# Decode attention with a gated MLP on one core: part of an output-weight block in eight-lane transfers, VectorE operations on whole K tiles

## The chip, the cores and the metric

The kernel runs on one core of a Trainium2 chip. The metric is the device time of one execution in microseconds (us); lower is better. A core has five engines that run side by side, each in the order of its own program: TensorE (PE, matmuls; PEld is its weight load), VectorE (DVE), ScalarE (ACT), GpSimd (POOL) and SyncE (SP), which here issues nearly all transfers. Sixteen DMA engines move data between HBM and SBUF, the on-chip memory of 128 partitions (lanes). Matmul results go to PSUM.

## The reference

For four sequences (B = 4) with one new token each: layer norm, attention over a cache of 4096 keys and values with 32 heads of 128 elements, and beside it a small gated MLP; both are added to the input.

```python
xn = _layernorm(x, axis=-1)
return x + _A_ref(xn, A_k_cache, A_v_cache, A_wq, A_wo) + _B_ref(xn, ...)

# _A_ref
q = (x @ wq).reshape(B, Sq, Hq, Dh).transpose(0, 2, 1, 3)
scores = jnp.einsum('bhqd,bhkd->bhqk', q, k) * Dh ** (-0.5)
p = _softmax(scores, axis=-1)
o = jnp.einsum('bhqk,bhkd->bhqd', p, v)
return o.transpose(0, 2, 1, 3).reshape(B, Sq, Hq * Dh) @ wo

# _B_ref
z = _gelu(jnp.einsum('bsd,df->bsf', x, w_in))
z2 = _layernorm(z[..., Fh:], axis=-1)
g = jnp.einsum('ts,bsf->btf', w_sp, z2) + b_sp[None, :, None]
return jnp.einsum('bsf,fd->bsd', z[..., :Fh] * g, w_out)
```

The caches are bfloat16, 4 x 32 x 4096 x 128 each: 134 MB of keys and 134 MB of values, all read once. wo is 4096 x 640.

## The kernel before

Four heads of one sequence make a tile: 4 x 4096 rows of 128 elements, laid out as 128 lanes x 128 rows x 128 elements (4 MB, 32 KB a lane). There are 32 K tiles and 32 V tiles. Tile i belongs to head group i // 4 (eight groups) and sequence i % 4. The main loop makes one turn per K tile.

**Loads.** Five SBUF slots (`KV_SLOTS`) hold K and V tiles. `pump` issues the next loads of a fixed list on SyncE's queue, which alternates V and K (twice, at turns 24 and 28, an extra K comes earlier). In turn i two loads are issued: the V tile that takes the slot freed by this turn's `blocks`, then the K tile that takes the slot freed by this turn's `sums`. SyncE waits for each slot in that order. The output weights wo come in eight blocks of 128 lanes x 2560 elements (5,120 bytes a lane); `load_wo` issues block i // 4 at the end of turns 2, 6, 10, 14, 18 and 22, behind that turn's V and K, and the last two after the loop. Two buffers hold them.

**A turn.** The order on PE, DVE, ACT and SP is written out by hand, and each engine follows it. For K tile i:

- `product` (VectorE, L457): the tile times the query, in place, in two halves of 64 rows of 128 elements (8192 elements a lane each).
- `fold_half` (VectorE, L466): adds the upper 64 elements of each row to the lower 64, for each half (4096 elements).
- `sums` (TensorE, L475): eight matmuls with the identity for each half, which add the 64 elements down to 8 in PSUM (`ps_s`, two buffers of one half each).
- `row_sums` (VectorE, L486): reduces these 8 to one score, for each half.

The second half's row sums are read in the next turn, behind that turn's first product. There also come, for tile i - 1: `lane_max` (VectorE, L495), `lay_max` (ScalarE, L501), `spread_max` (TensorE, L508), `head_max` (VectorE, L515, the negated maximum nb), and `exps`: an exponential on ScalarE (L524), then the product of the weights with a head mask on GpSimd (L533, tile pm, 512 elements a lane). Until turn 24 the V tile that is used in turn i is tile i - 1: `blocks` (TensorE, L548, 32 matmuls) multiplies pm with it. Behind every second tile come a copy to SBUF on ScalarE (L558) and `gather` (L569, eight small matmuls). On TensorE the second half's `sums` stand behind `blocks` and `gather`. From turn 26 on `blocks` is one turn further behind, in the last turn three.

When a head group is complete (turns 4, 8, ... 24), `group_den` (GpSimd L593, TensorE L600, VectorE reciprocal L602) and `group_norm` (VectorE, L607) work out the normalised output within that turn; on VectorE they stand ahead of the next turn's product. `group_turn`, `group_pick` (VectorE L627 and L635, next turn) and `group_proj` (L647) carry it through wo into `out_ps`, where the MLP's result is added too. The last V tile comes in four pieces, the last wo block in four.

VectorE's instructions of one turn, in order:

```python
product(i, 0); row_sums(i - 1, 1); lane_max(i - 1)
# group_pick of a group that the turn before has completed
fold_half(i, 0); head_max(i - 1)
product(i, 1)
# group_den's reciprocal
row_sums(i, 0); fold_half(i, 1)
# group_norm
```

Of the kernel before, what the change touches and what calls it, by code (L numbers as in the profile page):

```python
# [9 lines left out]
FP32 = mybir.dt.float32  # L10
BF16 = mybir.dt.bfloat16
ACT = mybir.ActivationFunctionType
ALU = mybir.AluOpType
AX = mybir.AxisListType

KV_SLOTS = 5
EXTRA_K = (24, 28)
ALIGN = 512


@with_exitstack
def kernel(
# [14 lines left out]
    nc = tc.nc  # L37
    P = nc.NUM_PARTITIONS
    Bsz, Sq, D = A_x.shape
    _, H, S, Dh = A_k_cache.shape  # L40
# [8 lines left out]
    HT = 4  # L49
    HG = H // HT  # L50
    NT = HG * Bsz
    LN = P // HT
    NC = HT * S // P
    HC = NC // 2
    HD2 = Dh // 2
    RW = 8
# [6 lines left out]

    skip = -(-(-nc.sbuf_base // 32) * 32) % ALIGN
    if skip:
        edge = ctx.enter_context(tc.tile_pool(name="edge", bufs=1))
        edge.tile([P, skip], mybir.dt.uint8, name="edge")
    kv = ctx.enter_context(tc.tile_pool(name="kv", bufs=KV_SLOTS))
    wop = ctx.enter_context(tc.tile_pool(name="wop", bufs=2))
    const = ctx.enter_context(tc.tile_pool(name="const", bufs=1))  # L70
    work = ctx.enter_context(tc.tile_pool(name="work", bufs=1))
    small = ctx.enter_context(tc.tile_pool(name="small", bufs=2))
    PSUM = bass.MemoryType.PSUM
    ps_s = ctx.enter_context(tc.tile_pool(name="ps_s", bufs=2, space=PSUM))
    ps_pv = ctx.enter_context(tc.tile_pool(name="ps_pv", bufs=2, space=PSUM))
    ps_m = ctx.enter_context(tc.tile_pool(name="ps_m", bufs=2, space=PSUM))
    ps_out = ctx.enter_context(tc.tile_pool(name="ps_out", bufs=1, space=PSUM))
# [2 lines left out]
    def slot(name):  # L80
        return kv.tile([P, SLOT], BF16, tag="kv", name=name)
# [8 lines left out]
    for c0, c1 in ((0, HT), (HT, DC)):  # L90
        t = slot("wq")[:, 0 : (c1 - c0) * HD].rearrange("p (c n) -> p c n", n=HD)
# [13 lines left out]
        out=w_out_sb[:, 0:NFF, :], in_=B_w_out[0 : NFF * P].rearrange("(p k) n -> p k n", k=NFF)  # L105
# [9 lines left out]
    k_tiles, v_tiles = {}, {}  # L115
# [24 lines left out]
    def pump():  # L140
        while n_loaded[0] < len(loads):
            at = n_loaded[0] + 3 - KV_SLOTS
            if at >= 0 and occupants[at] not in used:
                return
            load(*loads[n_loaded[0]])
            n_loaded[0] += 1


    wo_r = A_wo.rearrange("(j p r) n -> j p (r n)", p=P, r=HT)
    wo_h = A_wo.rearrange("(j h p) n -> j p h n", p=P, h=HT)  # L150
    wo_tiles = {}

    def load_wo(j):
        wo_tiles[j] = wop.tile([P, HT, D], BF16, name="wo")
        if j == HG - 1:
            for hh in range(HT):
                nc.sync.dma_start(out=wo_tiles[j][:, hh, :], in_=wo_h[j][:, hh, :])
            return
        nc.sync.dma_start(out=wo_tiles[j][:].rearrange("p r n -> p (r n)"), in_=wo_r[j])

    pump()

# [2 lines left out]
    ident = const.tile([P, P], BF16)  # L165
# [11 lines left out]
        out=lane_diag[:],  # L177
        in_=ident_f[:].rearrange("p (h l) -> p l h", h=HT),
        axis=AX.X,
        op=ALU.add,  # L180
# [12 lines left out]
    for e in range(2):  # L193
        nc.vector.tensor_reduce(
            out=sel[:, :, :, e],
            in_=ident_f[:].rearrange("p (g e k h) -> p e k h g", g=CG, e=2, k=GC)[:, e],
            axis=AX.X,
            op=ALU.add,
# [4 lines left out]
    for hh in range(HT):  # L203
# [3 lines left out]
        out=spread[:],  # L207
        in_=ident[:].rearrange("p (m r) -> p r m", r=HT)[:, :, None, :].to_broadcast(
            [P, HT, HT, LN]
        ),  # L210
# [5 lines left out]
        out=q_lanes[:].rearrange("r b (h l) -> r b h l", h=HT),  # L216
        in_=ident[: HT * Bsz, : HT * Bsz]
# [7 lines left out]
    for hh in range(HT):  # L225
        nc.gpsimd.tensor_copy(
            out=place[:, hh, hh * Bsz : (hh + 1) * Bsz], in_=lane_diag[:, 0:Bsz]
# [18 lines left out]
    for i in range(NSTAT):  # L246
# [5 lines left out]
        out=rstd[:], in_=mv[:, 1:2], func=ACT.Sqrt, bias=eps_tile[:Bsz], scale=1.0  # L252
# [4 lines left out]
        out=xn_bf[:],  # L257
# [9 lines left out]
    for c in range(DC):  # L267
        nc.tensor.transpose(
            out=xnT_ps[:, c, :], in_=xn_v[:, c, :], identity=ident[:Bsz, :Bsz]
# [11 lines left out]
    for c in range(DC):  # L281
        t, i = wq_parts[c]
        for hg in range(HG):
            g = hg % CG
            nc.tensor.matmul(  # L285
                out=q_ps[hg // CG][g * LN : (g + 1) * LN, :],
                lhsT=xnT[:, c, :],
                rhs=t[:, i, hg * HT * Dh : (hg + 1) * HT * Dh],
                start=(c == 0),
                stop=(c == DC - 1),  # L290
# [9 lines left out]
    def out_sum(half):  # L300
        return out_ps[OG * half : OG * half + Bsz, :]

    for half in range(2):
        nc.tensor.matmul(
            out=out_sum(half),
            lhsT=ident[:Bsz, :Bsz],
            rhs=x_bf[:, half * NOH : (half + 1) * NOH],
            start=True,
            stop=False,
# [121 lines left out]
    qbcs, scores, pvs, blocks_sb = {}, {}, {}, {}  # L431
    sums_ps, maxes = {}, {}
# [19 lines left out]
        qbcs[hg] = small.tile([P, Bsz, Dh], BF16, name="qbc")  # L452
        nc.scalar.copy(out=qbcs[hg][:], in_=qb_ps[:])

    def product(i, half):
        t = k_tiles[i][:, half * HC : (half + 1) * HC, :]
        nc.vector.tensor_tensor(  # L457
            out=t,
            in0=t,
            in1=qbcs[i // Bsz][:, i % Bsz, None, :].to_broadcast([P, HC, Dh]),  # L460
            op=ALU.mult,
        )

    def fold_half(i, half):
        t = k_tiles[i][:, half * HC : (half + 1) * HC, :]
        nc.vector.tensor_tensor(  # L466
            out=t[:, :, 0:HD2], in0=t[:, :, 0:HD2], in1=t[:, :, HD2:Dh], op=ALU.add
        )

    def sums(i, half):  # L470
        t = k_tiles[i][:, half * HC : (half + 1) * HC, :]
        s = sums_ps[i, half] = ps_s.tile([P, HC, RW], FP32, name="s_ps")
        n = HD2 // RW
        for g in range(n):
            nc.tensor.matmul(  # L475
                out=s[:],
                lhsT=ident[:],
                rhs=t[:, :, g * RW : (g + 1) * RW],
                start=(g == 0),
                stop=(g == n - 1),  # L480
            )

    def row_sums(i, half):
        if half == 0:
            scores[i] = small.tile([P, NC], FP32, name="s_sb")
        nc.vector.tensor_reduce(  # L486
            out=scores[i][:, half * HC : (half + 1) * HC],
            in_=sums_ps.pop((i, half))[:],
            axis=AX.X,
            op=ALU.add,  # L490
        )

    def lane_max(i):
# [161 lines left out]
    def group(i, fn):  # L655
        if 0 <= i < NT and i % Bsz == Bsz - 1:
            fn(i // Bsz)

    def at(i, fn, *args):
        if 0 <= i < NT:  # L660
            fn(i, *args)
# [10 lines left out]
    with tc.manual_schedule(engines={E.PE, E.DVE, E.Activation, E.SP}):  # L672
        stage_q(0)
        gmlp()
        used.update(occupants[:3])
        pump()
        for i in range(NT):
            j = turns.get(i)
            product(i, 0)
            at(i - 1, row_sums, 1)  # L680
            at(i - 1, lane_max)
            at(i - 1, lay_max)
            at(i - 1, spread_max)
            group(turns.get(i - 1, -1), group_pick)
            if turns.get(i - 1, -1) // Bsz < HG - 2:
                group(turns.get(i - 1, -1), group_proj)
            fold_half(i, 0)
            at(i - 1, head_max)
            at(i - 1, exps)
            sums(i, 0)  # L690
            product(i, 1)
            if i % Bsz == 2 and i // Bsz + 1 < HG:
                stage_q(i // Bsz + 1)
            due = [] if j is None else [j]
            if i == NT - 1:
                due += range(j + 1, NT - 2)
            for n, jj in enumerate(due):
                if n:
                    gather(due[n - 1])
                blocks(jj)  # L700
                group(jj, group_den)
                used.add(("v", jj))
            row_sums(i, 0)
            fold_half(i, 1)
            if due:
                gather(due[-1])
            for jj in due:
                group(jj, group_norm)
            sums(i, 1)
            for jj in due:  # L710
                group(jj, group_turn)
            used.add(("k", i))
            pump()
            if i % Bsz == 2 and i // Bsz < HG - 2:
                load_wo(i // Bsz)
        load_wo(HG - 2)
        load_wo(HG - 1)
        row_sums(NT - 1, 1)
        lane_max(NT - 1)
        lay_max(NT - 1)  # L720
        spread_max(NT - 1)
        head_max(NT - 1)
        exps(NT - 1)
        blocks(NT - 2)
        group_den(HG - 1)
        blocks(NT - 1, 0, V_CUTS[1])
        gather(NT - 1, stop=False)
        for c0, c1 in zip(V_CUTS[1:], V_CUTS[2:]):
            pairs(NT - 1, c0, c1)
        group_norm(HG - 1)  # L730
        group_proj(HG - 2)
        group_proj(HG - 1)

        res = work.tile([P, NOH], BF16, name="res")
        out_v = out.flatten_outer_dims()
        r0, r1 = slice(0, Bsz), slice(OG, OG + Bsz)
        nc.scalar.copy(out=res[r0], in_=out_ps[r0])
        nc.vector.tensor_copy(out=res[r1], in_=out_ps[r1])
        nc.scalar.dma_start(out=out_v[:, 0:NOH], in_=res[r0])
        nc.sync.dma_start(out=out_v[:, NOH:D], in_=res[r1])  # L740
# [30 lines left out]
```

## Time and profile before

| | |
|---|---|
| time, median of 3 runs | 663.49 us (663.44 to 663.57) |
| the profiled execution's own time | 663.4 us |
| its span, first to last instruction | 661.6 us |
| VectorE busy | 491.5 us (74%) |
| TensorE busy | 348.7 us (53%) |
| GpSimd busy | 151.3 us (23%) |
| ScalarE busy | 49.3 us (7%) |
| read from HBM | 282.24 MB, 427 GB/s over the span |
| mean granted TensorE clock | 0.726 |

Each line of a timeline gives start, duration, engine, source line, operation, output <- inputs, the shape (partitions x elements) and the count; square brackets give the engine's idle time before it and what ended it. A group line of the page gives busy time in all and the mean of one in ns, then the engine's idle time before these instructions and what ended most of it. In the row of forty digits each digit is the busy share, in tenths, of one fortieth of the span. A "q" behind an engine's name means its sequencer, which waits and issues transfers.

### The profile page before, as it was taken

What the parts mean: (1) busy time and instruction counts of PE and PEld (TensorE: products, weight loads), DVE (VectorE), ACT (ScalarE), POOL (GpSimd) and SP (SyncE); (2) the same over time, 40 slices, a digit from 0 to 9 for tenths busy, and PEclk for the clock granted to TensorE, in tenths of its full rate; (3) what the DMA queues carried; (4) which work ended last, traced back from release to release, by engine and by line L of the source; (5) the groups of instructions that cost most, each with busy time, mean ns of one, the idle gap of its engine ahead of it and who ended that gap; (6) DMA issues with size and microseconds to landing.
All of it is one profiled execution on the core that took longest, in us unless ns stands there. A gap on an engine that the chain in (4) does not pass through costs nothing.

```text
span 661.6 us, 5115 instructions
## 1 busy us (share of the span) xinstructions
PE 348.7 (53%) x2109; PEld 144.6 (22%) x2109; DVE 491.5 (74%) x334; ACT 49.3 (7%) x138; POOL 151.3 (23%) x57
## 2 busy tenths in 40 slices
PE   2526653646445455663745654465643756435567
PEld 1402211212121121221212222121211312112124
DVE  2299797867789677788776698776787899777950
ACT  0201100001000010001000000000100000000010
POOL 3002222112222112222112222112222133122230
PEclk9999676776767777766678657777576577688585
DMA  9999999999999999999999999999999999999997
GB/s 368 432 438 429 430 440 427 440 423 434 442 416 447 424 433 442 423 440 424 433 440 423 440 428 431 442 421 442 422 435 442 422 441 428 427 442 428 429 428 289
DMA packets 11971, 282.57 MB, mean 427 GB/s; under 512 B 1344, under 2 KB 1964, under 8 KB 3244
## 3 DMA queue, kind: packets, MB, share of 16 engines
q1 hardware_dynamic: 11928, 282.25, 99.2%
q8 instruction: 16, 0.26, 0.1%
q14 instruction: 7, 0.06, 0.0%
q10 hardware_dynamic: 20, 0.01, 0.0%
HBM read 282.24 MB, written 0.01 MB: 427 GB/s over the span
## 4 chain that ended last, share of the span: by engine, by line
issue 49%; DMA 25%; POOL 15%; DVE 7%; PE 3%; SPq 1%; ACT 0%; POOLq 0%; DVEq 0%; ACTq 0%
DMA k_nat<-in_A_k_cache_dram 20%; POOL pm L533 15%; DMA wo<-in_A_wo_dram 4%; DVE k_nat L457 4%; DVE k_nat L466 2%; PE s_ps L475 2%; PE pv_acc L548 1%; SPq L123 0%; DVE s_sb L486 0%; PE out_ps L647 0%; PE pv L569 0%; POOL own_sum L593 0%; DVE m L495 0%; SPq L92 0%; SPq L104 0%
## 5 line engine op out<-in xcount | busy, mean ns | idle before, releaser
L457 DVE TENSOR_TENSOR k_nat<-k_nat,qbc 128x8192 bf16<-128x8192 bf16 x64 | 282.8, 4419 | 97.8 <-DMA k_nat<-in_A_k_cache_dram 97.8
L533 POOL TENSOR_TENSOR pm<-p,hmask_bf 128x512 bf16<-128x512 bf16 x32 | 142.5, 4452 | 490.9 <-ACT p L524 490.9
L475 PE MATMUL s_ps<-k_nat,ident 128*128 128x512 bf16 x512 | 189.2, 536 | 68.2 <-DVE k_nat L466 68.2
L466 DVE TENSOR_TENSOR k_nat<-k_nat 128x4096 bf16<-128x4096 bf16 x64 | 151.8, 2372 | 0.0
L548 PE MATMUL pv_acc<-v_nat,pm 128*32 128x512 bf16 x1008 | 88.6, 514 | 39.1 <-POOL pm L533 35.5
L508 PE MATMUL max_ps<-lay,head_scale 128*128 128x32 f32 x64 | 18.7, 383 | 171.4 <-ACT lay L501 171.4
L475 PEld LDWEIGHTS <-ident 128*128 128x128 bf16 x512 | 67.9, 135 | 171.1 <-issue 153.8
L508 PEld LDWEIGHTS max_ps<-lay,head_scale 128*128 128x128 f32 x64 | 14.6, 284 | 186.0 <-ACT lay L501 186.0
L548 PEld LDWEIGHTS <-pm 128*32 128x32 bf16 x1008 | 30.2, 120 | 96.2 <-POOL pm L533 52.0
L486 DVE TENSOR_REDUCE s_sb<-s_ps 128x64 f32<-128x512 f32 x64 | 43.3, 677 | 4.2 <-PE s_ps L475 4.2
L501 ACT ACTIVATE lay<-lane_diag,m 128x32 f32<-128x32 f32 x32 | 10.3, 321 | 395.9 <-DVE m L495 395.9
L602 DVE RECIPROCAL rden<-den 128x16 f32<-128x16 f32 x8 | 2.1, 257 | 32.2 <-PE den L600 32.2
L569 PE MATMUL pv<-sel,pv_sb 128*128 128x8 f32 x128 | 19.4, 279 | 9.3 <-ACT pv_sb L558 9.3
L569 PEld LDWEIGHTS pv<-sel,pv_sb 128*128 128x128 f32 x128 | 17.9, 217 | 17.2 <-ACT pv_sb L558 17.2
L524 ACT ACTIVATE p<-s_sb,nb 128x128 bf16<-128x128 f32 x32 | 12.9, 402 | 63.5 <-DVE nb L515 63.5
L558 ACT COPY pv_sb<-pv_acc 128x512 f32<-128x512 f32 x16 | 9.4, 585 | 91.8 <-PE pv_acc L548 91.8
L495 DVE TENSOR_REDUCE m<-s_sb 128x1 f32<-128x128 f32 x32 | 9.1, 286 | 1.1
L285 PE MATMUL q_ps<-wq,xnT 128*32 128x512 bf16 x40 | 4.5, 631 | 8.3 <-DMA wq<-in_A_wq_dram 8.3
L647 PE MATMUL out_ps<-wo,o_r 128*4 128x320 bf16 x56 | 8.0, 433 | 0.3 <-DMA wo<-in_A_wo_dram 0.3
L292 DVE CAST q_sb<-q_ps 128x512 bf16<-128x512 f32 x1 | 0.7, 691 | 9.3 <-PE q_ps L285 9.3
L515 DVE TENSOR_REDUCE nb<-max_ps 128x1 f32<-128x32 f32 x32 | 5.9, 183 | 0.9 <-PE max_ps L508 0.9
L607 DVE TENSOR_TENSOR o_n<-pv,rden 128x16 bf16<-128x16 f32 x8 | 1.3, 168 | 6.7 <-PE pv L581 6.7
(94 smaller groups left out, 91.4 us busy)
## 6 DMA issues: line engine op xcount, KB each, us to landing
k_nat<-in_A_k_cache_dram SPq DMA_DIRECT2D x32, 4096.0 KB, 37.9
v_nat<-in_A_v_cache_dram SPq DMA_DIRECT2D x31, 4096.0 KB, 33.6
wo<-in_A_wo_dram SPq DMA_DIRECT2D x7, 640.0 KB, 38.1
wq<-in_A_wq_dram SPq DMA_DIRECT2D x1, 4096.0 KB, 12.8
w_sb<-in_B_w_in_dram SPq DMA_DIRECT2D x1, 2160.0 KB, 19.5
v_nat<-in_A_v_cache_dram SPq DMA_DIRECT2D x1, 2048.0 KB, 24.5
wq<-in_A_wq_dram SPq DMA_DIRECT2D x1, 1024.0 KB, 14.8
v_nat<-in_A_v_cache_dram SPq DMA_DIRECT2D x1, 1024.0 KB
```

The lines of the kernel that those rows point to most:

```text
L457: nc.vector.tensor_tensor(out=t, in0=t, in1=qbcs[i // Bsz][:, i % Bsz, None, :].to_broadcast([P, HC, Dh]), op=ALU.mult,)
L466: nc.vector.tensor_tensor(out=t[:, :, 0:HD2], in0=t[:, :, 0:HD2], in1=t[:, :, HD2:Dh], op=ALU.add)
L475: nc.tensor.matmul(out=s[:], lhsT=ident[:], rhs=t[:, :, g * RW : (g + 1) * RW], start=(g == 0), stop=(g == n - 1),)
L486: nc.vector.tensor_reduce(out=scores[i][:, half * HC : (half + 1) * HC], in_=sums_ps.pop((i, half))[:], axis=AX.X, op=ALU.add,)
L495: nc.vector.tensor_reduce(out=m1[:], in_=scores[i][:], axis=AX.X, op=ALU.max)
L501: nc.scalar.activation(out=d[:], in_=lane_diag[:], func=ACT.Copy, scale=maxes[i][:, 0:1])
L508: nc.tensor.matmul(out=ps[:], lhsT=head_scale[:], rhs=maxes[i][:], start=True, stop=True)
L524: nc.scalar.activation(out=p[:], in_=scores.pop(i)[:], func=ACT.Exp, bias=nb[:], scale=scale_qk, accum_out=acc[hg % NACC][:, b : b + 1],)
L533: nc.gpsimd.tensor_tensor(out=p_m[b][:, :, e : e + GC * HT].rearrange("p g (c h) -> p g c h", h=HT), in0=p[:].rearrange("p (g c) -> p g c" ...
L548: nc.tensor.matmul(out=pv_acc[g * LN : (g + 1) * LN, :], lhsT=pm[:, c // GC, :], rhs=v_nat[:, c : c + GC, :].rearrange("p c d -> p (c d)") ...
L558: nc.scalar.copy(out=pv_sb[:], in_=pv_acc[:])
L569: nc.tensor.matmul(out=pvs[hg][:, :, b - 1 : b + 1], lhsT=pv_sb[:, k * Dh : (k + 1) * Dh], rhs=sel[:, k, :, :], start=(k == 0), stop=stop ...
```

## The change

Three things change.

1. `product`, `fold_half` (now `fold`) and `row_sums` work on the whole tile: one product over 16384 elements a lane, one fold over 8192, one row sum over 1024. The sixteen `sums` matmuls of a tile stand together, behind `blocks` and `gather`, and write one PSUM tile (4 KB a lane) of which there is one buffer instead of two of half the size. All of a tile's row sums are read in the next turn, behind that turn's product.
2. Of wo block 2, 80 of the 128 lanes are loaded in ten transfers of eight lanes, one at the end of each of the turns 0 to 9, behind that turn's V and K. The other 48 lanes are loaded at the end of turn 10, where the whole block was.
3. wo has three buffers instead of two, since block 2 is being filled while blocks 0 and 1 are used.

```diff
+SMALL_WO, SMALL_LANES = 2, 80
...
-    wop = ctx.enter_context(tc.tile_pool(name="wop", bufs=2))
+    wop = ctx.enter_context(tc.tile_pool(name="wop", bufs=3))
...
-    ps_s = ctx.enter_context(tc.tile_pool(name="ps_s", bufs=2, space=PSUM))
+    ps_s = ctx.enter_context(tc.tile_pool(name="ps_s", bufs=1, space=PSUM))
...
+    def load_wo_rows(j, p0, p1):
+        if j not in wo_tiles:
+            wo_tiles[j] = wop.tile([P, HT, D], BF16, name="wo")
+        rows = wo_tiles[j][:].rearrange("p r n -> p (r n)")
+        nc.sync.dma_start(out=rows[p0:p1], in_=wo_r[j][p0:p1])
+
     def load_wo(j):
-        wo_tiles[j] = wop.tile([P, HT, D], BF16, name="wo")
+        if j not in wo_tiles:
+            wo_tiles[j] = wop.tile([P, HT, D], BF16, name="wo")
...
-        nc.sync.dma_start(out=wo_tiles[j][:].rearrange("p r n -> p (r n)"), in_=wo_r[j])
+        p0 = SMALL_LANES if j == SMALL_WO else 0
+        load_wo_rows(j, p0, P)
...
-    def product(i, half):
-        t = k_tiles[i][:, half * HC : (half + 1) * HC, :]
+    def product(i):
+        t = k_tiles[i]
...
-    def sums(i, half):
-        t = k_tiles[i][:, half * HC : (half + 1) * HC, :]
-        s = sums_ps[i, half] = ps_s.tile([P, HC, RW], FP32, name="s_ps")
+    def sums(i):
+        s = sums_ps[i] = ps_s.tile([P, NC, RW], FP32, name="s_ps")
         n = HD2 // RW
...
+        for half in range(2):
+            cs = slice(half * HC, (half + 1) * HC)
+            for g in range(n):
+                nc.tensor.matmul(
+                    out=s[:, cs, :],
+                    lhsT=ident[:],
+                    rhs=k_tiles[i][:, cs, g * RW : (g + 1) * RW],
...
-            product(i, 0)
-            at(i - 1, row_sums, 1)
+            product(i)
+            at(i - 1, row_sums)
             at(i - 1, lane_max)
...
-            fold_half(i, 0)
+            fold(i)
             at(i - 1, head_max)
             at(i - 1, exps)
-            sums(i, 0)
-            product(i, 1)
...
-            row_sums(i, 0)
-            fold_half(i, 1)
             if due:
                 gather(due[-1])
             for jj in due:
                 group(jj, group_norm)
-            sums(i, 1)
+            sums(i)
...
             used.add(("k", i))
             pump()
+            if i < SMALL_LANES // 8:
+                load_wo_rows(SMALL_WO, 8 * i, 8 * i + 8)
             if i % Bsz == 2 and i // Bsz < HG - 2:
                 load_wo(i // Bsz)
...
-        row_sums(NT - 1, 1)
+        row_sums(NT - 1)
```

More of the change, by code (lines that the diff above doesn't have):

```diff
@@ L459, in product, with fold @@
             in0=t,
-            in1=qbcs[i // Bsz][:, i % Bsz, None, :].to_broadcast([P, HC, Dh]),
+            in1=qbcs[i // Bsz][:, i % Bsz, None, :].to_broadcast([P, NC, Dh]),
             op=ALU.mult,
         )
-    def fold_half(i, half):
-        t = k_tiles[i][:, half * HC : (half + 1) * HC, :]
+    def fold(i):
+        t = k_tiles[i]
         nc.vector.tensor_tensor(
@@ L468, in fold_half, with row_sums @@
         )
-    def sums(i, half):
-        t = k_tiles[i][:, half * HC : (half + 1) * HC, :]
-        s = sums_ps[i, half] = ps_s.tile([P, HC, RW], FP32, name="s_ps")
+    def sums(i):
+        s = sums_ps[i] = ps_s.tile([P, NC, RW], FP32, name="s_ps")
         n = HD2 // RW
[L474 to L485, printed above, removed]
+        for half in range(2):
[5 more added lines that the diff above has]
+                    rhs=k_tiles[i][:, cs, g * RW : (g + 1) * RW],
+                    start=(g == 0),
+                    stop=(g == n - 1),
+                )
+    def row_sums(i):
+        scores[i] = small.tile([P, NC], FP32, name="s_sb")
         nc.vector.tensor_reduce(
[L487 to L490, printed above, removed]
+            out=scores[i][:], in_=sums_ps.pop(i)[:], axis=AX.X, op=ALU.add
         )
```

## The prediction

> **What bounds the kernel now.** I read the page first: the DMA row, the queue row, the costliest group of VectorE.
>
> ```profile
> span 661.6 us, 5115 instructions
> ...
> DMA  9999999999999999999999999999999999999997
> ...
> q1 hardware_dynamic: 11928, 282.25, 99.2%
> ...
> L457 DVE TENSOR_TENSOR k_nat<-k_nat,qbc 128x8192 bf16<-128x8192 bf16 x64 | 282.8, 4419 | 97.8 <-DMA k_nat<-in_A_k_cache_dram 97.8
> ```
>
> SyncE's queue has the 16 DMA engines busy for 99.2% of the span, in every slice but the last, and VectorE's idle time before its product ends with the landing of a K tile. The loads set the time; compute costs only where it starves them or stretches the ends. Then the timeline of turn 14 (window 300 to 350 us):
>
> ```profile
> 300.47 4.43 DVE L457 TENSOR_TENSOR k_nat<-k_nat,qbc 128x8192 bf16<-128x8192 bf16 x1 [5.56 <-DMA k_nat<-in_A_k_cache_dram]
> ...
> 305.73 2.28 DVE L466 TENSOR_TENSOR k_nat<-k_nat 128x4096 bf16<-128x4096 bf16 x1
> ...
> 307.93 0.18 DVE L515 TENSOR_REDUCE nb<-max_ps 128x1 f32<-128x32 f32 x1
> 308.03 4.42 DVE L457 TENSOR_TENSOR k_nat<-k_nat,qbc 128x8192 bf16<-128x8192 bf16 x1
> ...
> 308.78 4.56 POOL L533 TENSOR_TENSOR pm<-p,hmask_bf 128x512 bf16<-128x512 bf16 x1 [16.02 <-ACT p L524]
> ...
> 312.96 2.53 DVE L466 TENSOR_TENSOR k_nat<-k_nat 128x4096 bf16<-128x4096 bf16 x1
> ...
> 317.05 0.33 SPq L123 DMA_DIRECT2D v_nat<-in_A_v_cache_dram  x1
> ...
> 319.79 4.43 DVE L457 TENSOR_TENSOR k_nat<-k_nat,qbc 128x8192 bf16<-128x8192 bf16 x1 [4.30 <-DMA k_nat<-in_A_k_cache_dram]
> ...
> 323.01 0.33 SPq L123 DMA_DIRECT2D k_nat<-in_A_k_cache_dram  x1
> ```
>
> K tiles come 19.32 us apart and VectorE waits 4.30 us for the next. A V slot is reloaded when `blocks` ends, 16.58 us into the turn, a K slot when `sums` ends, at 22.54. The pm operation of GpSimd begins 0.75 us after a product and ends at 313.34, 0.98 us after that product has given way (308.03 + 4.33). The same operation with VectorE idle, at the end of GpSimd's timeline:
>
> ```profile
> 580.74 2.26 POOL L593 TENSOR_TENSOR own_sum<-acc,hmask 128x16 f32<-128x16 f32 x1
> ...
> 643.88 1.04 POOL L533 TENSOR_TENSOR pm<-p,hmask_bf 128x512 bf16<-128x512 bf16 x1 [9.10 <-ACT p L524]
> 644.87 0.22 POOL L593 TENSOR_TENSOR own_sum<-acc,hmask 128x16 f32<-128x16 f32 x1
> ```
>
> So pm needs about 1.0 us and is kept out until the product ends; own_sum (0.22 us) took 2.26 us beside a fold, and the fold at 312.96 took 2.53 instead of 2.28 us because pm was still running. [...]
>
> **The change, part by part.**
>
> *Fewer, longer VectorE instructions.* Product: 4.42 us for 8192 elements, fold: 2.28 for 4096, so (4.42 − 2.28)/4096 = 0.52 ns each and 0.14 us fixed. Whole tiles: product 8.70 us, fold 4.42, each followed 0.08 us before its end, hence 8.62 and 4.34. Row sums: 0.68 us for 512, lane max 0.29 for 128, 1.02 ns each: 1.20 for 1024, the next 1.24 after its start. Three overheads of about 0.14 us go per turn; VectorE waits for K anyway: 0.
>
> *Order within a turn* (P is the product's start). Row sums of the tile before at P+8.62, lane max 9.86, fold 10.07, negated max 14.41, pm 0.85 later (55.72 to 56.57 in turn 1) at 15.26. If the next K tile has not landed, VectorE is idle and pm ends at 16.30; `blocks` 16.36 to 19.96 (3.60 us), which frees the V slot; sixteen `sums` matmuls follow, 7.1 us at half clock (3.57 for eight) or 3.9 at full clock (1.97). K slot free: 27.1 at the latest in turns without gather, 29.7 with it (copy and gather, 515.12 to 517.74, 2.62). Against 22.54 that is up to 7 us later, V 3.4. In the list of DMA issues a K tile takes 37.9 us to land and a V tile 33.6, of which 9.7 is its own transfer (half of 19.32): at least 20 us of queue lie before each, so the DMA does not starve: 0.
>
> *The gate.* All this holds while pm starts before the next product, else pm waits for the whole product. I checked the closest places. (a) Ordinary turn: 19.32 − 15.26 = 4.1 us of room; after a turn with gather `sums` can end at 29.7, where row sums want it at 27.94: 2.3 left. (b) Start:
>
> ```profile
> 34.46 4.42 DVE L457 TENSOR_TENSOR k_nat<-k_nat,qbc 128x8192 bf16<-128x8192 bf16 x1 [3.44 <-DMA k_nat<-in_A_k_cache_dram]
> ...
> 63.44 4.43 DVE L457 TENSOR_TENSOR k_nat<-k_nat,qbc 128x8192 bf16<-128x8192 bf16 x1 [0.16 <-DMA k_nat<-in_A_k_cache_dram]
> ```
>
> 34.46 + 8.74 + 4.34 (tile 0, the first fold waits for the product's end) + 8.62 + 1.24 + 0.21 + 4.34 + 0.85 = 62.80: pm starts 0.64 us before K tile 2. (c) After every fourth turn, where VectorE holds back the next product for `group_norm`:
>
> ```profile
> 511.52 3.60 PE L548 MATMUL pv_acc<-v_nat,pm 128*32 128x512 bf16 x32 [1.76 <-POOL pm L533]
> 515.06 0.61 PE L600 MATMUL den<-own_sum,ones_sq 128*128 128x16 f32 x2
> ...
> 515.87 1.87 PE L569 MATMUL pv<-sel,pv_sb 128*128 128x8 f32 x8 [0.21 <-ACT pv_sb L558]
> ```
>
> Next product at 16.36 + 6.22 (511.52 to 517.74) + 0.14 = P+22.7, its pm 15.26 + 0.42 (two `group_pick` operations) later, P+38.4. Tile 14 follows tile 12 by 40.30 us (260.17 to 300.47), with the whole wo block 2 in between; less 80 of its 128 rows (0.95 us, below), 39.35: 0.95 us of room. Elsewhere the whole block stays: 1.9. The gate holds, by little.
>
> *The wo block.* Bytes stay. Ten more issues of 0.42 us (L159) on SyncE, each behind that turn's V and K issue; the next waits tens of microseconds: 0 (without that cover 0.42 each). What moves is the load per DMA engine: 282.25 MB / 16 in 0.992 × 661.6 us is 26.9 bytes per ns, a 5,120-byte row 0.19 us. The four-row x_bf transfer left 5 landing events in the trace, a 128-row one 16, so eight rows should use eight engines. These carry 10 + 48/16 = 13 rows instead of 8, the other eight 3: +0.95 and −0.95 us. The engines are never idle, so that stands at the end. The sixteen landings of the last wo transfer lie in two clusters: seven within 0.74 us of the first, nine 2.23 to 2.81 us after it. Eight engines do not fit into seven places, so one of the nine gets the load: the end moves by 2.23 + 0.95 − 2.81 = 0.37 to 0.95; I take 0.8, since several may. Bounds −0.95 (only late engines relieved) and +0.95. [...]
>
> *Tail.* Product 30 at 606.54, 31 at +14.9 = 621.5, kept-out pm 29 at 631.1, blocks, gather, last `sums` by 644.5 (now 641.05), pm 31 by 649; the first part of V tile 31 is awaited until 650.15: 0.
>
> Sum: 661.6 + 0.8 = 662.4 us span, 664.2 for its execution (663.4 profiled; median shown 663.49, 0.09 above).
>
> **Rivals.**
> *The gate closes.* pm waits for the next product, V and `sums` slip, the next row sums slip, and the following K tile is there too, so it stays closed through turn 24 (from 25 on `blocks` lags by two tiles). From row sums to row sums: 1.24 + 0.21 + 4.34 + 0.10 + 8.62 + 0.98 + 0.06 + 3.60 = 19.15, plus about 4.2 for `sums` (even tile) or 2.62 + 5.2 (odd); a `group_norm` turn, whose pm is free, 22.8. Four turns 23.3 + 23.3 + 27 + 22.8 = 96.4 against 79.0: 4.3 us a turn. From turn 13, 11 turns, 47 less the queue's start: about +40, 704. From turn 1, 24 turns, 103 less 10 to 15: about 754. It decides from 0.64 us at (b), 0.95 at (c), or if TensorE stays at half clock so that `sums` slip add up. Against: the margins are worked out at the slow end. For: they are small. [...]
> *No skew, or the late engines relieved.* Eight-row transfers use all engines, or the nine late ones are the others: 662.5 to 663.5. Against: five landings of four rows.
> *pm is slow, not kept out.* 4.56 us in every turn: 3.5 us more, turns alternate 19.2 and 22.8, some 2 us over the loads' 19.7, 24 turns less 22 of queue: about 680. Against: 1.04, if one row may count.
>
> **Numbers.** Forecast 65%, gate closed 15%, no skew or relief 15%, slow pm 5%. Own range of the forecast 663.5 to 665.2. To leave out no more than 2 in 10 the range runs from 662.3 to 690: gates closing late (turn 17 on: 8 × 4.3 less 8) are in, early ones out. 0.2% is 1.3 us, about what can be told from no change. Forecast: 0.55 within, 0.10 above (an eight-row transfer may cost more than its rows); no skew: 0.11 within, 0.04 faster; the others slower. Faster 0.04, same 0.66, slower 0.30.
>
> **What would show it.** pm near 1.0 us in most turns up to 24 and ending before the next product; product 8.7, fold 4.4; V issues some 20 us into a turn; DMA still 9 in all slices. Wrong if pm has a mean of 5 to 10 us, if VectorE waits for `sums`, if DMA slices fall to 8, or if the landings' two clusters do not move apart by about a microsecond.

## The result and the profile after

The changed kernel takes 669.66 us (median of 5 runs, 669.13 to 670.34), the kernel before on the same chip 663.57 (663.44 to 663.63). The ratio is 1.0093, 95% interval 1.0078 to 1.0108: 6.1 us slower, where the forecast had 0.8. The profiled spans say the same, 668.6 against 661.6 us (that execution took 670.34 us, the longest of the five). Now and then one execution of a kernel, of the kernel before too, is 4 to 5.5 us longer than the others; the times here are medians, which such an execution does not move, as it does the ratios.

From the page of the kernel after: span, busy share of the DMA engines and GB/s in 40 slices, SyncE's queue, and the groups of the product, the fold, pm and the row sums.

```profile
span 668.6 us, 5054 instructions
...
DMA  9999999999999999999999999999999999999995
GB/s 371 421 439 438 421 433 429 424 423 422 430 425 430 430 415 426 411 409 427 432 431 438 425 437 430 434 428 433 433 434 435 427 432 437 428 433 434 430 428 238
...
q1 hardware_dynamic: 12008, 282.25, 98.9%
...
L466 DVE TENSOR_TENSOR k_nat<-k_nat,qbc 128x16384 bf16<-128x16384 bf16 x32 | 278.3, 8697 | 93.0 <-DMA k_nat<-in_A_k_cache_dram 93.0
...
L475 DVE TENSOR_TENSOR k_nat<-k_nat 128x8192 bf16<-128x8192 bf16 x32 | 141.3, 4416 | 0.0
L539 POOL TENSOR_TENSOR pm<-p,hmask_bf 128x512 bf16<-128x512 bf16 x32 | 56.6, 1769 | 589.3 <-ACT p L530 574.2
...
L495 DVE TENSOR_REDUCE s_sb<-s_ps 128x128 f32<-128x1024 f32 x32 | 39.0, 1219 | 9.4 <-PE s_ps L485 9.4
```

From the page of the kernel before, two lines to set beside them:

```profile
GB/s 368 432 438 429 430 440 427 440 423 434 442 416 447 424 433 442 423 440 424 433 440 423 440 428 431 442 421 442 422 435 442 422 441 428 427 442 428 429 428 289
...
L533 POOL TENSOR_TENSOR pm<-p,hmask_bf 128x512 bf16<-128x512 bf16 x32 | 142.5, 4452 | 490.9 <-ACT p L524 490.9
```

VectorE is as forecast: 8.70 us a product, 4.42 a fold, and its idle time before a product still ends with a K tile. pm has a mean of 1.77 us where before had 4.45: 29 of the 32 take 1.04 us, and three, at 542, 557 and 629 us, where `blocks` lags further behind, begin 0.76 us or so after a product and take 8.83. Whole tiles alone, below, has the same three and loses nothing. So the compute side did what it should, and the loss is elsewhere. The DMA row seems to say that nothing happened: 9 in every slice but the last. The row under it tells the story: slices 15 to 18 move 415, 426, 411 and 409 GB/s, where before has 433, 442, 423 and 440. Busy engines can be slow engines.

Where this happens is read from windows cut at the same turns (3 to 6, 7 to 10, 11 to 14, 15 to 18, each from a product's start). Columns: stretch, length, busy time of PE, PEld, DVE, ACT, POOL with counts, granted clock, DMA share, GB/s. First the kernel before:

```profile
82.75:161.75 79.00, 42.31 (x240) 16.59 (x239) 60.28 (x36) 5.27 (x16) 18.42 (x5) 0.70 1.00 433
161.75:240.77 79.02, 39.83 (x241) 16.25 (x239) 60.38 (x37) 5.27 (x16) 18.42 (x5) 0.74 1.00 433
240.77:319.79 79.02, 42.24 (x234) 17.23 (x233) 60.38 (x36) 5.27 (x16) 18.42 (x5) 0.67 1.00 432
319.79:400.19 80.40, 44.76 (x244) 17.37 (x243) 60.38 (x37) 5.27 (x16) 18.42 (x5) 0.68 1.00 432
```

Then the kernel after:

```profile
83.14:163.69 80.55, 40.35 (x246) 17.27 (x238) 59.01 (x24) 5.19 (x17) 4.33 (x5) 0.67 1.00 426
163.69:245.05 81.36, 36.64 (x238) 15.99 (x238) 58.92 (x24) 5.14 (x16) 4.33 (x5) 0.71 1.00 426
245.05:326.54 81.49, 36.53 (x238) 16.14 (x238) 58.92 (x24) 5.16 (x16) 4.33 (x5) 0.71 1.00 421
326.54:405.49 78.95, 38.60 (x246) 17.22 (x238) 58.92 (x25) 5.16 (x16) 4.33 (x5) 0.69 1.00 433
```

Turns 3 to 14 are 1.55, 2.34 and 2.47 us longer, 6.4 in all, and those are the turns in which the pieces of wo block 2 are in the queue. VectorE does less in them than before (58.9 against 60.4 us), and the DMA share is 1.00 in both; only the bytes per microsecond fell. From turn 15 on the rate is that of before. The fourth stretch is 1.45 us shorter than before's only because one landing of before came late there: fifteen of the sixteen of K tile 17 are in by 358.42 us, the last comes at 359.99. The kernel after has a like step later, at V tile 26 (583.16 and 584.36). The landing times below show that the loss is not made good.

The trace also holds a record of each DMA packet, of which I counted the long ones. A row of 32 KB (one lane of a K or V tile) takes 1.21 us on its engine. Rows longer than 1.23 us between 30 and 655 us, and their excess over 1.21 us per engine:

```
before          20 rows   0.57 us per engine
after          295        4.88
```

In the kernel after they stand in bursts: 5 to 40 of them around each eight-lane transfer (206 around the ten, most of them 1.3 to 1.6 us long) and 71 around the 48-lane one (280 to 288 us, most of them 1.3 to 2.0 us). The rows of wo, 5 KB each and 0.20 us in before, are slower there too, 0.27 us in the mean of the 48-lane transfer; all of them together add 0.6 us per engine. The K and V landings run late by the same steps: 0.38 us at K tile 3, 0.96 at tile 5, 1.94 at 7, 3.70 at 10, 5.69 at 12, 6.75 at 14 behind the 48-lane transfer, 6.75 at the last landing of all (665.03 us).

### The profile page after: what moved, and what is told of

It is laid out like the page before. It is cut to its first block, busy times and chain, and to the rows that moved or that the text cites. A ratio compares the mean times of both kernels' runs of the same rounds, so it can differ in the third digit from the quotient of the medians.

```text
span 668.6 us, 5054 instructions
## 1 busy us (share of the span) xinstructions
PE 321.8 (48%) x2109; PEld 144.9 (22%) x2109; DVE 480.4 (72%) x238; ACT 48.4 (7%) x138; POOL 63.4 (9%) x57
## 4 chain that ended last, share of the span: by engine, by line
issue 62%; DMA 18%; DVE 9%; PE 7%; POOL 4%; ACT 1%; SPq 0%; POOLq 0%; ACTq 0%; DVEq 0%
DMA k_nat<-in_A_k_cache_dram 12%; DMA wo<-in_A_wo_dram 4%; DVE k_nat L466 4%; POOL pm L539 4%; PE s_ps L485 3%; DVE k_nat L475 3%; DMA wq<-in_A_wq_dram 2%; PE pv_acc L554 2%; DVE s_sb L495 1%; PE pv L575 1%; PE q_ps L294 1%; PE out_ps L653 0%; ACT p L530 0%; DVE m L501 0%; ACT pv_sb L564 0%
## 5 line engine op out<-in xcount | busy, mean ns | idle before, releaser
L466 DVE TENSOR_TENSOR k_nat<-k_nat,qbc 128x16384 bf16<-128x16384 bf16 x32 | 278.3, 8697 | 93.0 <-DMA k_nat<-in_A_k_cache_dram 93.0
L485 PE MATMUL s_ps<-k_nat,ident 128*128 128x512 bf16 x512 | 142.4, 441 | 20.9 <-DVE k_nat L475 20.9
L554 PE MATMUL pv_acc<-v_nat,pm 128*32 128x512 bf16 x1008 | 106.9, 600 | 91.7 <-POOL pm L539 90.7
L475 DVE TENSOR_TENSOR k_nat<-k_nat 128x8192 bf16<-128x8192 bf16 x32 | 141.3, 4416 | 0.0
L539 POOL TENSOR_TENSOR pm<-p,hmask_bf 128x512 bf16<-128x512 bf16 x32 | 56.6, 1769 | 589.3 <-ACT p L530 574.2
L485 PEld LDWEIGHTS <-ident 128*128 128x128 bf16 x512 | 56.0, 114 | 106.6 <-issue 59.2
L554 PEld LDWEIGHTS <-pm 128*32 128x32 bf16 x1008 | 33.8, 135 | 146.6 <-POOL pm L539 97.1
L495 DVE TENSOR_REDUCE s_sb<-s_ps 128x128 f32<-128x1024 f32 x32 | 39.0, 1219 | 9.4 <-PE s_ps L485 9.4
L458 PE MATMUL qbc_ps<-q_rows,q_lanes 16*128 16x128 bf16 x32 | 4.4, 284 | 26.1 <-ACT q_rows L455 26.1
L458 PEld LDWEIGHTS <-q_lanes 16*128 16x128 bf16 x32 | 3.1, 117 | 27.4 <-DVE nb L521 22.6
```

Source lines behind the costliest of these rows:

```text
L466: nc.vector.tensor_tensor(out=t, in0=t, in1=qbcs[i // Bsz][:, i % Bsz, None, :].to_broadcast([P, NC, Dh]), op=ALU.mult,)
L475: nc.vector.tensor_tensor(out=t[:, :, 0:HD2], in0=t[:, :, 0:HD2], in1=t[:, :, HD2:Dh], op=ALU.add)
L485: nc.tensor.matmul(out=s[:, cs, :], lhsT=ident[:], rhs=k_tiles[i][:, cs, g * RW : (g + 1) * RW], start=(g == 0), stop=(g == n - 1),)
L495: nc.vector.tensor_reduce(out=scores[i][:], in_=sums_ps.pop(i)[:], axis=AX.X, op=ALU.add)
L539: nc.gpsimd.tensor_tensor(out=p_m[b][:, :, e : e + GC * HT].rearrange("p g (c h) -> p g c h", h=HT), in0=p[:].rearrange("p (g c) -> p g c" ...
L554: nc.tensor.matmul(out=pv_acc[g * LN : (g + 1) * LN, :], lhsT=pm[:, c // GC, :], rhs=v_nat[:, c : c + GC, :].rearrange("p c d -> p (c d)") ...
```

## The experiments

Diffs are against the kernel after, where nothing else is said. Each ratio is to the kernel before in runs on the same chip. GB/s of two fixed stretches, 84 to 220 us (where most of the eight-lane transfers lie) and 220 to 300 us (the last ones and the rest of the block), is quoted for several of them; before has 433 and 434 there, after 426 and 417.

### Whole tiles alone

```diff
-SMALL_WO, SMALL_LANES = 2, 80
+SMALL_WO, SMALL_LANES = 2, 0
```

> The changed kernel with wo block 2 loaded in one transfer at turn 10 again: whole-tile product, fold and row sums alone. Theory A (all the loss is in the transfers of block 2, the whole tiles cost nothing because pm starts before the next product): 663.2 to 663.9 us, pm near 1.0 us in most turns. Rival C (the later release of the V and K slots, 20 and 25 us into a turn, feeds back into the loads): 665 to 669 us.

663.65 us, ratio 1.0019 (1.0001 to 1.0037; that of the medians is 1.0001); the profiled span is 661.8 us, 0.2 above before's. Its page has the whole-tile operations as in the kernel after, at the old rate:

```profile
q1 hardware_dynamic: 11928, 282.25, 99.2%
...
L466 DVE TENSOR_TENSOR k_nat<-k_nat,qbc 128x16384 bf16<-128x16384 bf16 x32 | 278.2, 8695 | 86.3 <-DMA k_nat<-in_A_k_cache_dram 86.3
...
L539 POOL TENSOR_TENSOR pm<-p,hmask_bf 128x512 bf16<-128x512 bf16 x32 | 56.6, 1769 | 581.5 <-ACT p L530 566.3
```

V and K slots come free about as late here as in the kernel after, and it costs nothing. This half of the change is worth 0, as forecast.

### The small transfers alone

Against the kernel before, with products, folds and row sums in halves as there:

```diff
+SMALL_WO, SMALL_LANES = 2, 80
...
-    wop = ctx.enter_context(tc.tile_pool(name="wop", bufs=2))
+    wop = ctx.enter_context(tc.tile_pool(name="wop", bufs=3))
...
+            if i < SMALL_LANES // 8:
+                load_wo_rows(SMALL_WO, 8 * i, 8 * i + 8)
```

> The kernel before with the ten eight-lane transfers and the 48-lane one, product, fold and row sums in halves as before. Theory A: 669 to 670.5 us, the whole loss. Rival C: 664 to 666 us, the skew of 0.4 to 1 us that was forecast and little more.

670.14 us, ratio 1.0099 (1.0086 to 1.0112), with 332 long rows. The whole loss sits in how block 2 is cut.

### Which lanes a small transfer writes

Two kernels that differ in nothing but the eight lanes of each small transfer. Both load the whole block at turn 10 as well, so that 64 of its rows come twice, and the large transfer is as before. The first takes neighbouring lanes:

```diff
-SMALL_WO, SMALL_LANES = 2, 80
+SMALL_WO, SMALL_LANES = 2, 64
...
-        p0 = SMALL_LANES if j == SMALL_WO else 0
-        load_wo_rows(j, p0, P)
+        load_wo_rows(j, 0, P)
```

> Changed kernel, block 2: eight transfers of eight lanes next to each other (lanes 0 to 63) in turns 0 to 7 and then the whole block of 128 lanes at turn 10, so 64 rows are loaded twice and no transfer of 48 lanes is left. The eight extra rows of 0.19 us on eight engines are 1.5 us of load, of which 0.9 to 1.5 should stand at the end. In the changed kernel's trace the K and V tiles land 5.88 us late by turn 12, 1.96 of it the ten rows: 0.39 us of disturbance for each small transfer, 3.1 for eight. Theory A and its rival B alike: 667 to 668.5 us.

The second, on top of that, takes lanes four apart:

```diff
-    def load_wo_rows(j, p0, p1):
+    def load_wo_rows(j, p0, p1, step=1):
...
-        nc.sync.dma_start(out=rows[p0:p1], in_=wo_r[j][p0:p1])
+        nc.sync.dma_start(out=rows[p0:p1:step], in_=wo_r[j][p0:p1:step])
...
-                load_wo_rows(SMALL_WO, 8 * i, 8 * i + 8)
+                p0 = i // 4 * 32 + i % 4
+                load_wo_rows(SMALL_WO, p0, p0 + 29, 4)
```

> As the run before, the same bytes in the same turns, but the eight lanes of a transfer lie four lanes apart (0, 4, ... 28 and so on) instead of next to each other. Theory A1 (a small transfer disturbs because its eight engines write into lanes that other engines are filling with K and V rows; four apart, each engine writes among the lanes that it fills anyway): no disturbance, only the load of 0.9 to 1.5 us, 664.3 to 665.2 us, and no slower K and V rows near the small transfers. Rival B (any small transfer on half of the engines puts them out of step, whichever lanes it writes): as with neighbouring lanes, 667 to 668.5 us. [...]

Neighbouring lanes: 667.45 us, ratio 1.0070 (1.0049 to 1.0091), span 665.5, 179 long rows. Four apart: 664.99 us, ratio 1.0031 (1.0016 to 1.0046), span 663.4, 20 long rows, exactly as many as before. The windows of 84 to 220 us, where six of the eight small transfers lie, of the first:

```profile
84.00:220.00 136.00, 63.90 (x386) 29.06 (x386) 101.77 (x42) 7.74 (x25) 6.58 (x8) 0.69 1.00 429
```

and of the second:

```profile
84.00:220.00 136.00, 66.83 (x390) 30.17 (x394) 102.04 (x43) 8.21 (x27) 7.62 (x9) 0.68 1.01 433
```

Same number of transfers, same bytes, same places in the queue: which eight lanes go together decides, 429 against 433 GB/s and 2.5 us of median time. (The rows of wo that are read from HBM go with the lanes, so no run separates the writing side from the reading side. That neighbouring rows are read cannot be enough, since one transfer of all 128 reads them too and leaves no more long rows than before: 20, on whole tiles alone.) What is left in the second, 1.34 us over whole tiles alone, is about the load itself: eight extra rows on each of eight engines, if they are the same eight each time, 8 × 0.19 = 1.5 us, 0.9 to 1.5 by the prediction's way of counting. The sixteen landings of its last transfer are 0.75 us later in the mean than before's, and 64 extra rows of 0.19 us over 16 engines are 0.76.

A small transfer leaves eight landing events behind a jump at its issue, where a 128-lane one leaves sixteen, so it is taken to run on eight of the sixteen engines. Which engine fills which lanes, no record shows: that lanes four apart lie among those that each engine fills anyway, and neighbouring ones do not, is the author's assumption in theory A1, above and below. The runs agree with it in which lanes cost (429 GB/s and 179 long rows for neighbouring ones) and which don't (433 and 20). They do not show the slowing to stay with eight engines: rows are in flight sixteen at a time (16.0 in the mean of 84 to 300 us), and around eight of the ten eight-lane transfers of the kernel after there is a moment when sixteen of the long K and V rows are in flight together. That the choice of lanes costs the time is shown; the mechanism is open.

### The same block in other pieces

At turn 10, block 2 in two transfers of 80 and 48 lanes, and nothing small:

```diff
-SMALL_WO, SMALL_LANES = 2, 80
+SMALL_WO, SMALL_LANES = 2, 0
...
-        p0 = SMALL_LANES if j == SMALL_WO else 0
+        p0 = 80 if j == SMALL_WO else 0
+        if p0:
+            load_wo_rows(j, 0, p0)
         load_wo_rows(j, p0, P)
```

> Whole tiles, block 2 at turn 10 in two transfers of 80 and 48 neighbouring lanes, no small ones; every byte is loaded once and every engine has 5 + 3 rows, as many as before. Theory A1 (rows that cross into the lanes of other engines disturb): in the changed kernel the 48-lane transfer took the landings from 5.88 us late with 1.96 us of load to 6.75 with 0.95, 1.9 us of disturbance for 3 rows an engine; with 5 rows more 3 to 5 us in all, 666 to 669 us. Rival B (half of the engines out of step): 663.2 to 663.9 us, since all sixteen carry the same.

666.71 us, ratio 1.0054 (1.0035 to 1.0072). One cut costs some 3 us over one transfer: 2.98 us above the kernel before on the same chip (663.73), where whole tiles alone was 0.08 above it on another chip. Its page has it in one slice, the 17th (266 to 283 us):

```profile
GB/s 371 425 438 434 423 438 437 426 435 438 426 426 445 422 441 436 370 423 426 433 434 430 435 436 431 429 437 428 434 437 430 434 435 430 431 436 434 427 430 275
```

370 for about 435 is a loss of 16.6 × 65/435 = 2.5 us there. The packets agree: 53 long K and V rows, 1.5 us per engine more than in before, and the 128 rows of this block take 0.35 us in the mean for 0.20, 1.2 us per engine. So it isn't smallness: 80 lanes are no small transfer.

Ten transfers in turns 0 to 9 again, each of all 128 lanes and 256 elements (512 bytes a row), and nothing at turn 10:

```diff
+    def load_wo_cols(j, c0, c1):
...
+        nc.sync.dma_start(out=rows[:, c0:c1], in_=wo_r[j][:, c0:c1])
...
-        p0 = SMALL_LANES if j == SMALL_WO else 0
-        load_wo_rows(j, p0, P)
+        if j != SMALL_WO:
+            load_wo_rows(j, 0, P)
...
-                load_wo_rows(SMALL_WO, 8 * i, 8 * i + 8)
+                load_wo_cols(SMALL_WO, 256 * i, 256 * i + 256)
```

> Whole tiles, block 2 in ten transfers in turns 0 to 9, each of all 128 lanes and a tenth of the columns (512 bytes a row). Theory A1: every engine writes its own lanes, no disturbance, 663.3 to 664.5 us (the shorter rows may take a little more). Rival D (each transfer more costs some 0.4 us, whatever its shape): 667 to 668 us.

664.29 us, ratio 1.0017 (1.0003 to 1.0031); 432 and 430 GB/s, and 20 long rows. Ten transfers in the same places cost 0.5 us over one (0.56 above the kernel before, for 0.08), not 6. So it isn't the number of transfers or of issues either.

Five transfers of 16 neighbouring lanes, then the 48:

```diff
-            if i < SMALL_LANES // 8:
-                load_wo_rows(SMALL_WO, 8 * i, 8 * i + 8)
+            if i < SMALL_LANES // 16:
+                load_wo_rows(SMALL_WO, 16 * i, 16 * i + 16)
```

> The changed kernel with the 80 lanes in five transfers of sixteen neighbouring lanes in turns 0 to 4, then the 48 lanes. [...] Theory A1: five disturbances of 0.4 to 0.8 us and 1.9 us of the 48-lane transfer, 667 to 669.5 us. Rival B: 663.2 to 664 us.

668.87 us, ratio 1.0102 (1.0072 to 1.0132; that of the medians is 1.0077); 425 GB/s in both stretches, 203 long rows. Each sixteen-lane transfer leaves sixteen landing events in the trace, so sixteen engines carry one row each and the load stays even: the landings of the last transfer lie 3.15 us apart, about as on whole tiles alone (3.11). The loss stays all the same, 5.1 us of the 6.1: uneven load is the small part of it.

### The gate, closed on purpose

The prediction's chief rival did not come. How near was it? On whole tiles alone, the lane max of turn 1 stands five times (the result is the same), 1.06 us in place of 0.29 ahead of pm:

```diff
-SMALL_WO, SMALL_LANES = 2, 80
+SMALL_WO, SMALL_LANES = 2, 0
...
-            at(i - 1, lane_max)
+            for _ in range(5 if i == 1 else 1):
+                at(i - 1, lane_max)
```

> Whole tiles, block 2 in one transfer, and in turn 1 alone the lane max is taken five times instead of once, some 1.1 us of VectorE in one turn of 32. pm of that turn then comes due after K tile 2 has landed (0.65 us of room in the changed kernel's trace: product at 63.53, pm from 62.86). Theory E (pm is kept out by the product for its whole length, and this sustains itself to turn 24): 735 to 765 us, pm some 9 us in three turns of four. Rival F (pm is only slow beside a product, 4.56 us): at most 670 us. Rival G (one late turn is caught up): 663.5 to 665 us.

758.13 us, ratio 1.1414 (1.1399 to 1.1429). The timeline of turns 1 and 2 in the kernel after, where the gate holds:

```profile
62.01 0.18 DVE L521 TENSOR_REDUCE nb<-max_ps 128x1 f32<-128x32 f32 x1
...
62.87 1.04 POOL L539 TENSOR_TENSOR pm<-p,hmask_bf 128x512 bf16<-128x512 bf16 x1 [54.72 <-ACT p L530]
63.53 8.93 DVE L466 TENSOR_TENSOR k_nat<-k_nat,qbc 128x16384 bf16<-128x16384 bf16 x1 [1.34 <-DMA k_nat<-in_A_k_cache_dram]
```

and in this kernel:

```profile
62.53 0.18 DVE L521 TENSOR_REDUCE nb<-max_ps 128x1 f32<-128x32 f32 x1
...
63.28 8.69 DVE L466 TENSOR_TENSOR k_nat<-k_nat,qbc 128x16384 bf16<-128x16384 bf16 x1 [0.57 <-DMA k_nat<-in_A_k_cache_dram]
63.39 9.48 POOL L539 TENSOR_TENSOR pm<-p,hmask_bf 128x512 bf16<-128x512 bf16 x1 [54.59 <-ACT p L530]
72.93 3.60 PE L554 MATMUL pv_acc<-v_nat,pm 128*32 128x512 bf16 x32 [13.60 <-POOL pm L539]
...
80.56 1.22 DVE L495 TENSOR_REDUCE s_sb<-s_ps 128x128 f32<-128x1024 f32 x1 [8.58 <-PE s_ps L485]
```

In the first, pm starts 0.66 us ahead of the product, and the product is the longer for it (8.93 for 8.69 us). In the second it starts 0.11 us behind, runs 9.48 us, `blocks` follows at 72.93, and the next row sums wait 8.58 us for `sums`, so that the next pm is late too. From there it feeds itself. Two groups of its page:

```profile
L466 DVE TENSOR_TENSOR k_nat<-k_nat,qbc 128x16384 bf16<-128x16384 bf16 x32 | 277.8, 8681 | 4.3 <-DMA k_nat<-in_A_k_cache_dram 4.3
...
L539 POOL TENSOR_TENSOR pm<-p,hmask_bf 128x512 bf16<-128x512 bf16 x32 | 213.1, 6659 | 520.6 <-ACT p L530 506.2
```

VectorE waits for K tiles no more (4.3 us in all, for 86.3), and pm's mean is 6.66 us: 23 of the 32 take 8.8 to 9.5 us, for three on whole tiles alone. The prediction's price for a gate closed from turn 1, about 754 us, was right to 4 us.

### The rare long runs

> Kernels with whole tiles show, in 10 of the 56 runs so far, a time 4 to 5.5 us above their own median; before and the kernel with halves have none such. Here the lane max of turn 27 stands nine times (same output), so that the pm of tile 26 starts about 1.7 us later, 0.6 us behind the start of product 28, where the kernel with whole tiles and the block in one transfer had it 1.1 us ahead. Theory H: the rare runs are those in which this late gate closes. Then nearly every run here is at 667 to 669.5. Theory I: a gate closed so late costs nothing, since the last loads set the end, and the rare runs have another cause. Then 663.4 to 664.5, with the same few runs above.

> The kernel with whole tiles and the block in one transfer again, with nothing changed, for a trace of one of its rare runs at 667.9 to 668.9 (3 of 12). If it is one: by theory H the pm of tile 26 starts behind product 28 and takes over 8 us; by I all pm as before and a stretch in which the loads move fewer bytes. If it is not one, it tells nothing.

> As the run before it: a second chance of a trace of one of the rare runs.

The first is the diff of the experiment above with `9 if i == 27`. 663.63 us, ratio 1.0 (0.9975 to 1.0024); two of its ten executions were longer, 668.0 and 678.11 us. Its timeline shows the gate closed in turn 28, as meant:

```profile
568.08 8.69 DVE L466 TENSOR_TENSOR k_nat<-k_nat,qbc 128x16384 bf16<-128x16384 bf16 x1 [0.39 <-DMA k_nat<-in_A_k_cache_dram]
...
568.35 9.31 POOL L539 TENSOR_TENSOR pm<-p,hmask_bf 128x512 bf16<-128x512 bf16 x1 [7.90 <-ACT p L530]
```

That execution took 663.74 us, so theory H fell: a gate closed this late costs nothing. The other two kernels (663.85 and 663.75 us, one execution each) tell nothing. The kernel before, beside them, had 669.03 and 677.04 us among thirteen executions, so the whole tiles are not needed for it. What makes the rare long executions is open.

## Why the prediction was right, and where it was wrong

*What bounds the kernel.* Right: loads do. The test named for it was the wrong one: the DMA share stayed at 9, while the rate fell.

*Fewer, longer VectorE instructions.* Right: 8.70 and 4.42 us, worth 0, hidden by the wait for K; whole tiles alone shows it.

*Order within a turn.* Right. pm was forecast 15.26 us behind the product's start, with 1.04 us of its own; in turn 6 of the kernel after the product starts at 143.86 us and pm at 159.10, 15.24 later, for 1.04 us; the V slot's reload is issued at 163.60, 19.7 us into the turn, and the DMA engines never ran dry.

*The gate.* Right, and with the margins that were worked out: 62.80 forecast for pm in turn 1, 62.87 measured, 0.66 us ahead of the product for a forecast 0.64. Behind turn 13, where 0.95 us was worked out, there were 3.8 us (pm at 303.41, product at 307.22), since the slow transfers made tile 14 later; whole tiles alone had 2.6 (297.99 and 300.57). The forecast of 15% for the closed gate stands on 0.64 us, and the experiment that took these away shows that the price was no exaggeration.

*The wo block.* Here the sum failed. "The engines are never idle, so that stands at the end" and "the end moves by 2.23 + 0.95 − 2.81 = 0.37 to 0.95; I take 0.8" gave the only term, counting each engine's own rows and nothing that they do to others. A cost of that kind is there: with lanes four apart and eight extra rows, 1.34 us. That the ten transfers use the same eight engines each time, on which the 0.95 rests, no run shows; the runs show the landings of the last wo transfer 5.48 us apart behind ten eight-lane transfers, 3.15 behind five of sixteen lanes, 2.81 before. But the transfers cost 6.1 us, of which the greater part is rows slowed beside them, which the sum put at nothing: at the measured rates 136 × (1 − 426/433) + 80 × (1 − 417/434) = 2.2 + 3.1 = 5.3 us between 84 and 300 us. The landings of the last transfer divide it up: in the mean of the sixteen they are 4.98 us late, though the load per engine is the same in the mean, and the packets have 4.3 us of slowed K and V rows and 0.5 of slowed wo rows per engine for it; the last landing is 6.75 us late, so that unevenness has 1.8, where the forecast had 0.8 for it and for the whole. The case was named, "an eight-row transfer may cost more than its rows", with 10% and without a price. It could have been bounded from the transfers of before only badly, as every large one of them has 128 lanes.

*Two clusters of landings.* They moved apart more than forecast, and are two no longer: the sixteen landings of the last wo transfer lie 5.48 us apart, for 2.81 before, spread over the whole of it.

*The tail.* Right: the compute after the loads adds nothing. The last landing is 6.75 us late (665.03 for 658.28), and the span ends 3.5 us behind it, where before it was 3.3.

The range held, by the room that it left for a gate closed late. That is luck: the time came from another cause. No run closes the gate from turn 17, which that room was for; closed in turn 28, it cost nothing.

## What to carry to other kernels

A transfer that was put among others was cheap here only in two shapes: cut a block by columns of all 128 lanes (ten pieces for 0.5 us), or take lanes four apart, not runs of neighbouring ones (0.3 us for each eight-lane piece, by 667.45 − 664.99 over eight; some 3 us for one cut into 80 and 48). Read GB/s by slice, not the busy share of the DMA engines, since a slowed engine counts as busy (here a 9 in slices of 409 to 426 GB/s). And where a VectorE product is made longer, look for a GpSimd operation that starts close ahead of it: 0.8 us here was worth 94.

## What was not expected of the hardware

Eight rows of 5 KB are 0.19 us for each of eight engines, yet such a transfer of neighbouring lanes left 5 to 40 K and V rows longer than 1.23 us for 1.21, 0.06 to 0.48 us per engine and 0.27 in the mean of the ten. The 48-lane transfer left 71, 1.7 us per engine.

The exclusion of GpSimd by a product was all or nothing here: pm 0.66 us ahead runs 1.04 us, 0.11 us behind 9.48, 0.27 us behind 9.31. Where pm was first, the product took longer (8.93 us for 8.69). What keeps the later one out, no record shows.
